# The value at the centre as a column of the slopes' products, two groups' sums taken from PSUM products, and later loads of output weights and queries

## The chip, the cores and the metric

The kernel runs on one core of one Trainium2 chip. The metric is the time of the slowest core on the device, in microseconds (us); here there is only one core. A program has five engines that are used: TensorE (PE, matrix products into PSUM), VectorE (DVE), ScalarE (ACT), GpSimd (POOL) and SyncE (SP, which here only starts transfers). Each engine takes its instructions in the order in which the program holds them, so one that waits holds up all behind it on that engine. Times are those of one profiled execution, unless "runs" are named.

## The reference

The keys and values are one array: `kv` is averaged over 4x4 places (768 keys of 128 channels for each of 4 batches) and multiplied by `w_sr`. Attention runs over 12288 queries a batch, and a feed-forward network follows:

```python
kv_flat = kv_pool.reshape(B, -1, C) @ w_sr          # k = v = kv_flat
s = scale * (q @ k.transpose(0, 2, 1))
a = softmax(s)                                      # over 768 keys
x = a @ v                                           # 49152 tokens x 128
h = x @ w_in                                        # 2048 wide
out = (h - tanh(h)) @ w_out
```

## The kernel before

The outputs of the attention lie close to the mean of the values, so the kernel expands about it. For each batch it pools the keys, takes their mean (the centre, `cen`), and expands `h - tanh(h)` about the centre's `h`: a constant `G0` (128 numbers), a linear part `A` (128x128, "slopes"; kept as an upper and a lower half, `Ah`), and a cubic part of 16 tiles (`Wr` from the output weights, `winr` from the input weights). These come from `about_centre`, once a batch: `first` multiplies the centre by the input weights, a chain of small instructions on a 128x16 tile (`hb`) gives the functions' derivatives, `value` sums G0 (16 products with one column each), `by_first` scales the output weights by the first derivative on POOL (tile `Wg`, four of 128x512), `slopes` multiplies them with the turned input weights `winT` (16 products of 128x128), and `by_third` makes `Wr`.

The tokens go in 96 groups of 512 (24 a batch). For a group, `attention` computes the scores of 768 keys in three parts of 256 (PE into a two-bank tile `big`; ACT takes the exponential, tile `E`; DVE takes off 1 and the score, which leaves a small remainder `r2` in 16 bits). The sum of the three remainders over the keys is needed for the softmax's denominator. It is formed in SBUF by transfers: SP copies the first remainder into `rs` (`copied`), and POOL issues two adding transfers into it (`added`), each waiting for the landing of the one before. Two products with a tile of ones (`shares`) then sum over the keys into a PSUM bank, ACT turns that into the share left (`t`), PE forms the numerator (`straight` and `values`), DVE multiplies (`apart`, tile `df`), and POOL rounds it (`rounded`, tile `dr`). `feed_forward` multiplies `dr` by `winr` (`forth`, eight times two products), ACT squares, DVE cubes (one of eight on ACT and POOL instead), and `back` sums with `Wr`; `result` adds G0.

PSUM is divided into three two-bank tiles `big`, one bank `acc` and one bank `x`. The bank `x` is passed round between the denominator, the numerator and all the small products of `about_centre` and `keys`.

At the start, weights arrive as 64-bit words and are put together on ACT and DVE (`words_of`, eight times 512 KB: four for the input weights `i`, four for the output weights `o`), the first batch's keys arrive in 12 loads of 512 KB (`keys`, pooled by DVE, every third by POOL), and queries in loads of 256 KB. All these are issued by SP. Later batches' keys are gathered by adding transfers during earlier groups.

The order on each engine is not that of the code: every step is entered by `plan.op` with a step number, an engine, an estimated duration, and what it reads and writes, and `Plan.run` builds the order from these. Marks such as `first.{g}` are tiles without memory: they order steps in the plan and put no wait of their own into the program.

Of the kernel before, what the change touches and what calls it, by code (L numbers as in the profile page):

```python
# [21 lines left out]
P = 128  # L22
# [134 lines left out]
def attention_then_ffn(ctx: ExitStack, tc: tile.TileContext, q, kv_by_key, kv_by_place, w_sr, w_in,  # L157
# [18 lines left out]

    BUFS = {"kc": 2, "kvp": 1, "kTr": 2, "vvr": 2, "Mn": 1, "Mh": 2, "A": 2, "Ah": 2, "Wg": 3, "Wr": 2,
            "winr": 2, "q": 4, "qr": 5, "ql": 2, "E": 2, "r2": 7, "rs": 3, "t": 2, "dl": 1, "df": 1, "dr": 2, "u": 3, "r": 4,
            "rp": 2, "v": 2, "z": 1, "o": 2, "row": 2, "col": 2, "G0": 2, "hb": 2, "W2": 1,
# [53 lines left out]
    def words_of(step, load_step, n, kind):  # L233
# [56 lines left out]
        plan.op(load_step, "SP", 0.5, load_words, (), (words,), late=2.0, dma=1.27)  # L290
# [8 lines left out]
    def weights(step, load_step, out_step, load_out):  # L299
# [3 lines left out]
        for n in range(NW):  # L303
            words_of(out_step + n / 8, load_out + n / 8, n, "o")
# [46 lines left out]
    def keys(b, s0):  # L351
# [17 lines left out]
        for j in range(0 if b else NK):  # L369
# [9 lines left out]
            if j % 3 == 2:  # L379
                for k, w in enumerate((8, 4, 2, 1)):  # L380
                    def fold(key=key, w=w, at=at):
                        x = plan[key]
                        to = plan[kvp][:, at].unsqueeze(2) if w == 1 else x[:, :, 0:w]
                        PL.tensor_tensor(out=to, in0=x[:, :, 0:w], in1=x[:, :, w : 2 * w], op=ALU.add)

                    plan.op(s + k / 8, "POOL", 0.2 + KB * w * 0.0021, fold, (key,),
                            ((kvp, j),) if w == 1 else (key,))
            else:
                def pool(key=key, at=at):
                    V.tensor_reduce(out=plan[kvp][:, at], in_=plan[key], op=ALU.add, axis=AX.X)  # L390

                plan.op(s, "DVE", 1.2, pool, (key,), ((kvp, j),))
# [107 lines left out]
    def about_centre(b, s0):  # L500

        cen, hb, G0, Am, Wr, winr = (f"{x}.{b}" for x in ("cen", "hb", "G0", "A", "Wr", "winr"))
        ph, pg, pa = (f"{x}.{b}" for x in ("ph", "pg", "pa"))
# [5 lines left out]
        sb(G0, "G0", [P, 1])  # L509
# [4 lines left out]
        FS, CS, AS, APART, SA, VA, TA, WI, WS = EARLY if b < 2 else LATER  # L514
# [4 lines left out]
        value_at = [known + VA + AS * n if b else n / 2 + VL for n in range(4)]  # L519
        third_at = [known + TA + AS * (n + 0.5) if b else n / 2 - THIRD for n in range(4)]  # L520
        for n in range(4):
            if b or n == 0:
                bank(f"{ph}.{n}", "x" if b else "acc", first_at[n])
            if b:
                bank(f"{pg}.{n}", "x", value_at[n])
                bank(f"{pa}.{n}", "x", slopes_at[n] + APART)
        if not b:
            bank(f"{pa}.0", "acc", slopes_at[0])
            bank(f"{pg}.0", "acc", value_at[0])
# [69 lines left out]
        def sum_value(n):  # L599
            if n:  # L600
                V.tensor_tensor(out=plan[G0], in0=plan[f"{pg}.{n}"][:, 0:1], in1=plan[G0], op=ALU.add)
            else:
                V.tensor_scalar(out=plan[G0], in0=plan[f"{pg}.{n}"][:, 0:1], scalar1=1.0,
                                scalar2=None, op0=ALU.mult)

# [20 lines left out]
        for n in range(4):  # L626
            plan.op(value_at[n], "PE", 0.9, partial(value, n), (gg, ("wout32", n)),
                    (f"{pg}.{n if b else 0}",), late=0.2)
            if b:
                plan.op(value_at[n], "DVE", 0.15, partial(sum_value, n), (f"{pg}.{n}",), (G0,))  # L630
        if not b:
            plan.op(value_at[3], "DVE", 0.15, partial(sum_value, 0), (f"{pg}.0",), (G0,))
# [28 lines left out]
        else:  # L661
            for j in range(2):
                pw = f"pw.{b}.{j}"
                big(pw, winr_at + j / 2)
                for k in range(2):
                    dg = f"dg.{b}.{j}.{k}"
                    sb(dg, "Wg", [P, FW, C], step=winr_at + j / 2 + k / 4)
                    fs = slice((2 * j + k) * FW, (2 * j + k + 1) * FW)

                    def diagonal(j=j, dg=dg, fs=fs):  # L670
                        by = x(8)[:, fs].unsqueeze(2).to_broadcast([P, FW, P])
                        of = ident.unsqueeze(1).to_broadcast([P, FW, P])
                        (PL if j else V).tensor_tensor(out=plan[dg], in0=of, in1=by, op=ALU.mult)

                    def scaled(j=j, k=k, dg=dg, pw=pw):
                        for n in range(FW):
                            f = (2 * j + k) * FW + n
                            at = (k * FW + n) * P
                            PE.matmul(out=plan[pw][:, at : at + P], lhsT=winT[:, f], rhs=plan[dg][:, n],
# [10 lines left out]
        for n in range(NW):  # L690
            wg = f"wg.{b}.{n}"
            fs = slice(n * FW, (n + 1) * FW)
            sb(wg, "Wg", [P, FW, C], step=slopes_at[n])

            def by_first(n=n, wg=wg, fs=fs):
                by = x(4)[:, fs].unsqueeze(2).to_broadcast([P, FW, C])
                PL.tensor_tensor(out=plan[wg], in0=wout32[:, fs], in1=by, op=ALU.mult)

            def slopes(n=n, wg=wg):
                for k in range(FW):  # L700
                    PE.matmul(out=plan[f"{pa}.{n if b else 0}"][:, 0:P], lhsT=winT[:, n * FW + k],
# [3 lines left out]
            def sum_slopes(n=n):  # L705
                of = plan[f"{pa}.{n}"][:, 0:P]
                if n:
                    V.tensor_tensor(out=plan[Am], in0=of, in1=plan[Am], op=ALU.add)
                else:
                    A.copy(out=plan[Am], in_=of)  # L710
# [5 lines left out]
            plan.op(slopes_at[n], "POOL", 1.1, by_first, (gg, ("wout32", n)), (wg,), late=MORE if b else 0.0)  # L716
            joined = slopes_at[n] + (APART if b else SD)
            plan.op(joined, "PE", 0.95, slopes, (wg, "winT"), (f"{pa}.{n if b else 0}",), late=0.2)
            if b and n:
                plan.op(joined, "DVE", 0.29, sum_slopes, (f"{pa}.{n}",), (Am,), late=0.1)  # L720
            elif b or n == 3:
                plan.op(joined, "ACT", 0.3, partial(sum_slopes, 0), (f"{pa}.0",), (Am,), late=0.1)
# [11 lines left out]
        plan.op(joined, "ACT", 0.3, upper_slopes, (Am,), (Ah,), late=0.1)  # L734
# [14 lines left out]
    def attention(g, s0):  # L749
# [21 lines left out]
        behind = (f"first.{g - ago}",) if g >= ago + 3 else ()  # L771
# [25 lines left out]
        sb(rs, "rs", [P, WIDE], F16, step=s0 + AT["copied"])  # L797
# [45 lines left out]
        plan.op(s0 + AT["copied"], "SP", 0.5, copied, (r2s[0],), (rs,), late=2.0, dma=0.6)  # L843
        plan.tile(f"first.{g}", f"first.{g}", 1, lambda: None)
        for k in range(1, AN):
            to = (rs, f"first.{g}") if k == 1 else (rs,)
            plan.op(s0 + AT["added"][k - 1], "POOL", 0.87, partial(added, k), (r2s[k],), to,
                    late=2.4, dma=0.6, lane=True)
        plan.op(s0 + AT["shares"], "PE", 0.455, shares, ("ident", rs), (den,), late=0.196, lane=True)
# [17 lines left out]
    EARLY = (4, 1.6, 7, 3, 5, 4, 9, 18, 8)  # L867
    LATER = (8, 8, 9, 7, 16, 8, 32, 28, 8)
# [3 lines left out]
    def feed_forward(g, s0):  # L872
        b = g // NG
        Ah, Wr, G0, winr, dl, dr = (f"{x}.{k}" for x, k in (
            ("Ah", b), ("Wr", b), ("G0", b), ("winr", b), ("dl", g), ("dr", g)))
# [66 lines left out]
        def result():  # L942
            A.activation(out=plan[o], in_=plan[acc], func=AF.Identity, bias=plan[G0])  # L943
# [4 lines left out]
        plan.op(s0 + AT["result"], "ACT", 0.565, result, (acc, G0), (o,), late=0.16, lane=True)  # L948
# [202 lines left out]
    weights(-LEAD - 50, -LEAD - 60, -17.7, -LEAD - 46)  # L1151
# [4 lines left out]
    VL = -10  # L1156
# [74 lines left out]
```

## Time and profile before

| | us |
|---|---|
| runs, median of 3 | 1346.77 (1346.31 to 1349.07) |
| the profiled execution, its own time | 1346.26 |
| its span in the profile | 1344.5 |
| results of groups 2 to 11, apart | 12.57 each |
| first score product of group 0 begins | 51.19 |
| first `forth` product of group 0 begins | 78.03 |

The span begins with the first instruction and ends with the last; 1.76 us of the execution's own time lie around it. Line numbers are those of the kernel before. A row of the timeline gives the start, the stretch in us, the engine, the line, the operation, what it writes and reads, and how many; in brackets is the idle time of the engine before it and what ended that. Matmul records come two to a product where both sides are f32, one otherwise. The clock column PEclk gives TensorE's granted clock as a share of 2.4 GHz (0.50 is 1.2 GHz).

### The profile page before, as it was taken

Reading aid. Unit: us, or ns where it says so; the run is one execution under the profiler, and the core shown is the slowest. Engines: PE = TensorE matmul, PEld = TensorE weight load, DVE = VectorE, ACT = ScalarE, POOL = GpSimd, SP = SyncE. Lnnn points to the kernel's source line nnn. Section 1 sums busy time; section 2 is a strip of 40 time slices with the busy share of each in tenths; the row PEclk is TensorE's granted clock in tenths of the full one; section 3 lists DMA queues with packets and bytes.
Section 4 is the critical chain, followed back from the end, with each engine's and each line's share of the span. In section 5 each row is a group of like instructions: output and inputs, shape, how many; then the busy total and the mean of one; then the engine's idle time right before and its main releaser. Section 6 shows DMA issues by size and latency. Waiting matters only on the chain.

```text
span 1344.5 us, 17619 instructions
## 1 busy us (share of the span) xinstructions
PE 1279.7 (95%) x5632; PEld 899.7 (67%) x5632; DVE 1221.3 (91%) x1214; ACT 1195.9 (89%) x1403; POOL 1147.4 (85%) x973
## 2 busy tenths in 40 slices
PE   2889999899999999999999999999999999999997
PEld 2657666577666667776666666777676667666664
DVE  6578999888899999998999999899999999899996
ACT  5378999888899999898999999889899999899995
POOL 2568999779999998799999998889998888798896
PEclk7989999999999999999999999999999999999999
DMA  8165666435566664444566664344444444444431
GB/s 345 46 122 119 139 140 132 104 98 135 125 130 138 141 131 109 99 118 107 128 139 132 138 141 114 95 105 109 110 101 104 117 104 102 101 102 106 114 85 35
DMA packets 83574, 160.07 MB, mean 119 GB/s; under 512 B 10032, under 2 KB 12208, under 8 KB 83472
## 3 DMA queue, kind: packets, MB, share of 16 engines
q0 software_dynamic: 34128, 68.04, 31.0%
q1 hardware_dynamic: 49344, 90.81, 19.3%
q8 instruction: 46, 0.75, 0.2%
q14 instruction: 56, 0.46, 0.1%
HBM read 57.93 MB, written 25.39 MB: 62 GB/s over the span
## 4 chain that ended last, share of the span: by engine, by line
PE 45%; POOL 39%; ACT 5%; issue 5%; DMA 3%; DVE 2%; SPq 0%; POOLq 0%; ACTq 0%; DVEq 0%
PE acc L932 13%; PE big L894 12%; POOL rp L912 9%; POOL z L912 9%; PE big L783 6%; POOL rs L805 5%; PE x L825 5%; POOL z L908 4%; POOL ql L819 3%; POOL dr L839 3%; ACT E L787 3%; PE x L815 2%; PE acc L883 2%; POOL dl L863 2%; DMA rs<-r 1%
## 5 line engine op out<-in xcount | busy, mean ns | idle before, releaser
L901 DVE SCALAR_TENSOR_TENSOR r<-big,u 128x1024 fp32r<-128x1024 f32 x672 | 780.6, 1218 | 33.6 <-ACT u L898 32.0
L898 ACT ACTIVATE u<-big 128x1024 f32<-128x1024 f32 x672 | 661.9, 1034 | 45.1 <-PE big L894 34.6
L894 PE MATMUL big<-dr,winr 128*128 128x512 f32 x1536 | 509.6, 413 | 2.5 <-DVE r L790 1.6
L932 PE MATMUL acc<-r,Wr 128*128 128x512 f32 x1344 | 424.7, 408 | 0.7 <-DVE r L901 0.7
L790 DVE SCALAR_TENSOR_TENSOR r<-E,big 128x1024 f16<-128x1024 f32 x288 | 350.3, 1218 | 47.9 <-ACT E L787 44.5
L894 PEld LDWEIGHTS big<-dr,winr 128*128 128x128 f32 x1536 | 275.3, 189 | 97.6 <-DVE r L790 23.1
L787 ACT ACTIVATE E<-big 128x1024 f32<-128x1024 f32 x288 | 295.8, 1029 | 18.7 <-PE big L783 11.4
L932 PEld LDWEIGHTS acc<-r,Wr 128*128 128x128 f32 x1344 | 251.6, 188 | 64.1 <-DVE r L901 1.6
L912 POOL TENSOR_TENSOR rp<-z,v 128x1024 fp32r<-128x1024 f32 x96 | 273.1, 2845 | 0.2
L912 POOL TENSOR_TENSOR z<-z,v 128x1024 f32<-128x1024 f32 x96 | 247.6, 2579 | 4.3
L805 POOL DMA_DIRECT2D rs<-r x192 | 226.4, 1179 | 11.6 <-DMA rs<-r 9.6
L783 PE MATMUL big<-qr,kTr 128*128 128x512 f32 x576 | 196.5, 424 | 1.6 <-ACT v L905 1.6
L839 POOL TENSOR_SCALAR dr<-df 128x512 fp32r<-128x512 f32 x96 | 68.7, 715 | 128.7 <-DVE df L836 92.6
L825 PE MATMUL x<-r,vvr 128*128 128x512 f16 x576 | 176.3, 389 | 0.0
L819 POOL TENSOR_TENSOR ql<-q,qr 128x512 fp32r<-128x512 f32 x96 | 165.0, 1719 | 0.0
L863 POOL TENSOR_TENSOR dl<-df,dr 128x512 fp32r<-128x512 f32 x96 | 164.2, 1711 | 0.0
L783 PEld LDWEIGHTS big<-qr,kTr 128*128 128x128 f32 x576 | 105.5, 190 | 42.9 <-DVE r L790 15.4
L908 POOL TENSOR_SCALAR z<-v 128x1024 f32<-128x1024 f32 x96 | 109.7, 1143 | 0.0
L905 ACT COPY v<-big 128x1024 f32<-128x1024 f32 x96 | 97.6, 1017 | 1.1 <-PE big L894 1.0
L943 ACT ACTIVATE o<-acc,G 128x512 f32<-128x512 f32 x96 | 65.7, 684 | 25.4 <-PE acc L932 24.3
L932 PE MATMUL acc<-rp,Wr 128*128 128x512 f32 x192 | 74.6, 469 | 13.9 <-POOL rp L912 10.1
L825 PEld LDWEIGHTS <-vvr 128*128 128x128 f16 x576 | 33.9, 99 | 79.5 <-issue 79.5
(183 smaller groups left out, 1023.4 us busy)
## 6 DMA issues: line engine op xcount, KB each, us to landing
rs<-r POOLq DMA_DIRECT2D x192, 256.0 KB, 3.9
q<-in_q_dram SPq DMA_DIRECT2D x96, 256.0 KB
rs<-r SPq DMA_DIRECT2D x96, 256.0 KB
out_dram<-o SPq DMA_DIRECT2D x96, 256.0 KB
kvp<-in_kv_by_place_dram POOLq DMA_DIRECT2D x45, 384.0 KB, 4.9
r<-in_kv_by_key_dram SPq DMA_DIRECT2D x6, 512.0 KB
kc<-inverse SPq DMA_DIRECT2D x12, 256.0 KB
u<-in_moe_w_in_dram SPq DMA_DIRECT2D x3, 512.0 KB
```

Source lines behind the costliest of these rows:

```text
L783: PE.matmul(out=half(plan[s], h), lhsT=plan[kTr][:, n * P : (n + 1) * P], rhs=plan[qr], start=True, stop=True)
L787: A.activation(out=plan[e], in_=plan[s], func=AF.Exp)
L790: V.scalar_tensor_tensor(out=plan[r], in0=plan[e], scalar=-1.0, in1=plan[s], op0=ALU.add, op1=ALU.subtract)
L805: PL.dma_start(out=plan[rs], in_=plan[r2s[k]], accum_op=ALU.add)
L819: PL.tensor_tensor(out=plan[ql], in0=plan[qs], in1=plan[qr].bitcast(F32), op=ALU.subtract)
L825: PE.matmul(out=plan[num], lhsT=plan[vvr][:, n], rhs=half(plan[f"r2.{g}.{k}"], h), start=(start and h == 0), stop=(stop and h == 1))
L863: PL.tensor_tensor(out=plan[dl], in0=plan[df], in1=plan[dr].bitcast(F32), op=ALU.subtract)
L894: PE.matmul(out=half(plan[hp], h), lhsT=plan[winr][:, f * P : (f + 1) * P], rhs=plan[dr], start=True, stop=True)
L898: A.activation(out=plan[u], in_=plan[hp], func=AF.Square)
L901: V.scalar_tensor_tensor(out=plan[r], in0=plan[hp], scalar=1.0, in1=plan[u], op0=ALU.add, op1=ALU.mult)
L912: PL.tensor_tensor(out=plan[to], in0=plan[x], in1=plan[y], op=ALU.mult)
L932: PE.matmul(out=plan[acc], lhsT=plan[Wr][:, 2 * n + h], rhs=half(plan[r], h), start=(start and h == 0), stop=(stop and h == 1))
```

## The change

Three edits, all in how the work is cut and ordered.

1. `value` and `sum_value` are gone. `by_first` now scales `winT` instead of the output weights, into tiles `Wg` with rows of 129; the 129th column holds the value function (`beside`, a copy of 128x4 on ACT). `slopes` multiplies with the output weights on the stationary side, so that its products of 128x129 hold the turned slopes and G0 in one tile `At`; a product with the identity (`turn_slopes`) turns the slopes back.
2. Groups 0 and 1 (`DIRECT = 2`) have no `rs`: `shares` runs over the three remainders themselves, six products instead of two.
3. The loads of the output weights and of the first queries stand behind the mark `held`, which the pooling of key load 6 writes; `out_weights` is entered after the keys of batch 0.

```diff
+    DIRECT, HELD = 2, 6
...
-        plan.op(load_step, "SP", 0.5, load_words, (), (words,), late=2.0, dma=1.27)
+        plan.op(load_step, "SP", 0.5, load_words, () if kind == "i" else ("held",), (words,), late=2.0,
+                dma=1.27)
...
-                plan.op(s, "DVE", 1.2, pool, (key,), ((kvp, j),))
+                plan.op(s, "DVE", 1.2, pool, (key,), ((kvp, j), "held") if j == HELD else ((kvp, j),))
...
-        def value(n):
-            for f in range(4 * n, 4 * n + 4):
-                PE.matmul(out=plan[f"{pg}.{n if b else 0}"][:, 0:1], lhsT=wout32[:, f],
-                          rhs=x(3)[:, f : f + 1], start=(f % (4 if b else FT) == 0),
-                          stop=(f % 4 == 3 and (b > 0 or n == 3)))
...
-            sb(wg, "Wg", [P, FW, C], step=slopes_at[n])
+            sb(wg, "Wg", [P, FW, C + 1], step=slopes_at[n])
...
-                PL.tensor_tensor(out=plan[wg], in0=wout32[:, fs], in1=by, op=ALU.mult)
+                PL.tensor_tensor(out=plan[wg][:, :, 0:C], in0=winT[:, fs], in1=by, op=ALU.mult)
+
+            def beside(wg=wg, fs=fs):
+                A.copy(out=plan[wg][:, :, C], in_=x(3)[:, fs])
...
-                    PE.matmul(out=plan[f"{pa}.{n if b else 0}"][:, 0:P], lhsT=winT[:, n * FW + k],
+                    PE.matmul(out=plan[f"{pa}.{n if b else 0}"][:, 0 : C + 1], lhsT=wout32[:, n * FW + k],
...
+        def turn_slopes():
+            PE.matmul(out=plan[pt][:, 0:P], lhsT=plan[At][:, 0:C], rhs=ident, start=True, stop=True)
+
         def upper_slopes():
+            A.copy(out=plan[Am], in_=plan[pt][:, 0:P])
             A.copy(out=plan[Ah][:, 0], in_=plan[Am])
...
-        behind = (f"first.{g - ago}",) if g >= ago + 3 else ()
+        behind = ("held",) if g < ago + 3 else (f"first.{g - ago}",)
...
         def shares():
-            for h in range(2):
-                PE.matmul(out=plan[den], lhsT=share, rhs=half(plan[rs], h), start=(h == 0),
-                          stop=(h == 1))
+            of = [rs] if g >= DIRECT else r2s
+            for n in range(2 * len(of)):
+                PE.matmul(out=plan[den], lhsT=share, rhs=half(plan[of[n // 2]], n % 2),
+                          start=(n == 0), stop=(n == 2 * len(of) - 1))
...
+        if g >= DIRECT:
+            plan.op(s0 + AT["copied"], "SP", 0.5, copied, (r2s[0],), (rs,), late=2.0, dma=0.6)
...
-            A.activation(out=plan[o], in_=plan[acc], func=AF.Identity, bias=plan[G0])
+            A.activation(out=plan[o], in_=plan[acc], func=AF.Identity, bias=plan[At][:, C : C + 1])
...
-    weights(-LEAD - 50, -LEAD - 60, -17.7, -LEAD - 46)
+    weights(-LEAD - 50, -LEAD - 60)
+    plan.tile("held", "held", 1, lambda: None)
...
+        if b == 0:
+            out_weights(-17.7, -LEAD - 46)
```

The order moves in two places. On SP, at the start, this stood before (`in_moe_w_out` are the output weights, `in_q` the queries, `in_kv_by_key` the keys of batch 0, `in_kv_by_place` the first gather of batch 1's keys):

```order
L376 DMA kc<-in_kv_by_key_dram 128x1024
L249 DMA u<-in_moe_w_out_dram 128x4x256
L249 DMA z<-in_moe_w_out_dram 128x4x256
L765 DMA q<-in_q_dram 128x512 x3
L249 DMA u<-in_moe_w_out_dram 128x4x256
L765 DMA q<-in_q_dram 128x512
L249 DMA u<-in_moe_w_out_dram 128x4x256
L376 DMA E<-in_kv_by_key_dram 128x1024
L376 DMA r<-in_kv_by_key_dram 128x1024 x2
L364 DMA kvp<-in_kv_by_place_dram 128x768
```

and this stands there now:

```order
L380 DMA kc<-in_kv_by_key_dram 128x1024
L380 DMA E<-in_kv_by_key_dram 128x1024
L380 DMA r<-in_kv_by_key_dram 128x1024 x2
L250 DMA u<-in_moe_w_out_dram 128x4x256 x3
L250 DMA z<-in_moe_w_out_dram 128x4x256
L756 DMA q<-in_q_dram 128x512 x5
L368 DMA kvp<-in_kv_by_place_dram 128x768
```

The last three key loads have moved ahead of four loads of output weights and four of queries. On PE, from the slopes of batch 0 to the first `values` product of group 0 (`x` is the bank for the denominator, then for the numerator), this stood before:

```order
L783 MATMUL big<-qr,kTr 128x512 x6
L701 MATMUL acc<-Wg,winT 128x128 x16
L809 LDWEIGHTS share
L809 MATMUL x<-rs,share 128x512
L809 LDWEIGHTS share
L809 MATMUL x<-rs,share 128x512
L815 MATMUL x<-qr,Mh 128x512 x2
```

and this stands there now:

```order
L685 MATMUL acc<-Wg,wout_69 128x129 x4
L774 MATMUL big<-qr,kTr 128x512 x2
L802 LDWEIGHTS share
L802 MATMUL x<-r_392,share 128x512
L802 LDWEIGHTS share
L802 MATMUL x<-r_392,share 128x512
...
L802 LDWEIGHTS share
L802 MATMUL x<-r_398,share 128x512
L685 MATMUL acc<-Wg,wout_69 128x129 x8
L808 MATMUL x<-qr,Mh 128x512 x2
```

The shares read the remainders (`r_392`, `r_380`, `r_398`) and no transfer's tile, and twelve of the sixteen slope products now stand behind the score products of group 1 or behind the shares.

## Rows read from the trace of the kernel before

**Rows 1.** SP's timeline at the start (start, stretch, engine, line, operation)
```profile
22.06 0.33 SPq L376 DMA_DIRECT2D E<-in_kv_by_key_dram  x1
```
**Rows 2.** Timeline of DVE and POOL: the last key loads as they land
```profile
20.67 1.22 DVE L390 TENSOR_REDUCE kvp<-kc 128x64 f32<-128x1024 f32 x1 [0.46 <-DMA kc<-in_kv_by_key_dram]
...
29.93 1.22 DVE L390 TENSOR_REDUCE kvp<-E 128x64 f32<-128x1024 f32 x1
...
32.56 2.52 POOL L384 TENSOR_TENSOR r<-r 128x512 f32<-128x512 f32 x3 [9.96 <-DVE kvp L390]
...
36.23 0.15 DVE L429 TENSOR_SCALAR row<-row 128x1 f32<-128x1 f32 x1
```
**Rows 3.** PE's timeline from the keys to the centre's products
```profile
31.30 6.45 PE L410 MATMUL big<-kvp,ident 128*128 128x512 f32 x10 [13.27 <-DVE kvp L390]
...
38.11 3.73 PE L535 MATMUL acc<-col,win 128*128 128x1 f32 x32 [0.25 <-DVE col L439]
```
**Rows 4.** Timeline of all engines: group 0's scores, remainders, and their sum by transfers
```profile
51.19 0.72 PE L783 MATMUL big<-qr,kTr 128*128 128x512 f32 x2
...
54.83 2.35 DVE L790 SCALAR_TENSOR_TENSOR r<-E,big 128x1024 f16<-128x1024 f32 x2 [0.60 <-ACT E L787]
...
57.81 3.73 PE L701 MATMUL acc<-Wg,winT 128*128 128x128 f32 x32
...
59.99 1.02 POOL L805 DMA_DIRECT2D rs<-r  x1
...
65.36 0.88 POOL L805 DMA_DIRECT2D rs<-r  x1 [2.63 <-DMA rs<-r]
...
68.78 1.01 PE L809 MATMUL x<-rs,share 128*128 128x512 f16 x2 [7.25 <-DMA rs<-r]
```
**Rows 5.** The same timeline, on to group 0's first `forth` product
```profile
71.94 2.78 PE L825 MATMUL x<-r,vvr 128*128 128x512 f16 x6
...
74.83 0.69 DVE L836 TENSOR_TENSOR df<-x,t 128x512 f32<-128x512 f32 x1 [13.12 <-PE x L825]
...
75.61 0.62 POOL L839 TENSOR_SCALAR dr<-df 128x512 fp32r<-128x512 f32 x1 [6.30 <-DVE df L836]
...
78.03 0.70 PE L894 MATMUL big<-dr,winr 128*128 128x512 f32 x2 [1.22 <-DVE r L790]
```
**Rows 6.** Stretches: length, busy of PE, PEld, DVE, ACT, POOL, then clock, transfers
```profile
45.50:65.80 20.30, 15.93 (x127) 14.99 (x126) 9.69 (x15) 10.91 (x15) 13.70 (x15) 1.00 0.25 72
...
65.90:76.10 10.20, 6.63 (x15) 3.35 (x15) 0.69 (x1) 1.60 (x3) 3.90 (x5) 0.50 0.64 117
```
**Rows 7.** Chain of waits: start, length, engine, what; two products at full clock
```profile
84.18 0.45 PE x L825 x2
```
**Rows 8.** Groups by line: putting weights together on DVE (busy, mean ns)
```profile
L275 DVE SCALAR_TENSOR_TENSOR wout<-u,v 128x512 int32<-128x512 int32 x3 | 2.1, 691 | 0.1
...
L268 DVE TENSOR_SCALAR v<-v 128x512 f32<-128x512 f32 x8 | 3.4, 421 | 7.4 <-ACT v L265 7.4
```
**Rows 9.** Forms of lines L673, L697, L655: count, then ns min/median/max
```profile
L673 DVE TENSOR_TENSOR Wg<-ident,hb x2: 693/1112/1530, 45.0 to 45.6; 128x512 f32<-128x512 f32 x2
...
L697 POOL TENSOR_TENSOR Wg<-wout,hb x16: 1037/1418/1839, 54.1 to 945.6; 128x512 f32<-128x512 f32 x16
...
L655 POOL TENSOR_TENSOR winr<-win,kc x12: 1856/2168/2623, 331.3 to 959.8; 128x512 fp32r<-128x512 f32 x12
```
**Rows 10.** Groups by line, batches 1 to 3: `value`'s products, a small copy
```profile
L595 PE MATMUL x<-hb,wout 128*128 128x1 f32 x96 | 11.9, 245 | 0.6 <-DVE df L836 0.4
...
L710 ACT COPY A<-x 128x128 f32<-128x128 f32 x3 | 0.8, 267 | 1.1 <-PE x L701 1.1
```
**Rows 11.** Stretches, as in rows 6: one group of batch 1's preparation
```profile
346.80:362.20 15.40, 14.08 (x69) 10.31 (x68) 13.17 (x14) 12.46 (x15) 15.40 (x15) 1.00 0.59 128
```
**Rows 12.** DVE's timeline: the longest row of cubes between two other instructions
```profile
1037.38 8.06 DVE L901 SCALAR_TENSOR_TENSOR r<-big,u 128x1024 fp32r<-128x1024 f32 x7
```

More of the change, by code (lines that the diff above doesn't have):

```diff
@@ L297, in words_of, with out_weights, weights @@
         plan.op(step, "DVE", 0.66, add, (part, rs), (part,), port=True)
-    def weights(step, load_step, out_step, load_out):
+    def out_weights(step, load_step):
+        for n in range(F // WN):
+            words_of(step + n / 8, load_step + n / 8, n, "o")
+    def weights(step, load_step):
         NW = F // WN
@@ L625, in about_centre @@
             plan.op(s0 - 5, on, 1.1, third_order, (hb,), (hb, a3s))
[L626 to L632, printed above, removed]
         NW, FW = 4, FT // 4
@@ L678, in scaled @@
                             at = (k * FW + n) * P
-                            PE.matmul(out=plan[pw][:, at : at + P], lhsT=winT[:, f], rhs=plan[dg][:, n],
+                            PE.matmul(out=plan[pw][:, at : at + P], lhsT=winT[:, f], rhs=plan[dg][:, n, 0:C],
                                       start=True, stop=True)
@@ L705, in sum_slopes @@
             def sum_slopes(n=n):
-                of = plan[f"{pa}.{n}"][:, 0:P]
+                of = plan[f"{pa}.{n}"][:, 0 : C + 1]
                 if n:
-                    V.tensor_tensor(out=plan[Am], in0=of, in1=plan[Am], op=ALU.add)
+                    V.tensor_tensor(out=plan[At], in0=of, in1=plan[At], op=ALU.add)
                 else:
-                    A.copy(out=plan[Am], in_=of)
+                    A.copy(out=plan[At], in_=of)
             def by_third(n=n, fs=fs):
@@ L714, in by_third @@
                 PL.tensor_tensor(out=plan[Wr][:, fs], in0=wout32[:, fs], in1=by, op=ALU.mult)
-            plan.op(slopes_at[n], "POOL", 1.1, by_first, (gg, ("wout32", n)), (wg,), late=MORE if b else 0.0)
+            plan.op(slopes_at[n], "POOL", 1.1, by_first, (gg, "winT"), ((wg, 0),), late=MORE if b else 0.0)
+            plan.op(slopes_at[n], "ACT", 0.2, beside, (gg,), ((wg, 1),), late=0.1)
             joined = slopes_at[n] + (APART if b else SD)
-            plan.op(joined, "PE", 0.95, slopes, (wg, "winT"), (f"{pa}.{n if b else 0}",), late=0.2)
+            plan.op(joined, "PE", 1.0, slopes, (wg, ("wout32", n)), (f"{pa}.{n if b else 0}",), late=0.2)
             if b and n:
-                plan.op(joined, "DVE", 0.29, sum_slopes, (f"{pa}.{n}",), (Am,), late=0.1)
+                plan.op(joined, "DVE", 0.29, sum_slopes, (f"{pa}.{n}",), (At,), late=0.1)
             elif b or n == 3:
-                plan.op(joined, "ACT", 0.3, partial(sum_slopes, 0), (f"{pa}.0",), (Am,), late=0.1)
+                plan.op(joined, "ACT", 0.3, partial(sum_slopes, 0), (f"{pa}.0",), (At,), late=0.1)
             plan.op(third_at[n], "POOL", 1.25, by_third,
                     (a3s, ("wout32", n)), ((Wr, n),), port=True)
+        def turn_slopes():
+            PE.matmul(out=plan[pt][:, 0:P], lhsT=plan[At][:, 0:C], rhs=ident, start=True, stop=True)
         def upper_slopes():
+            A.copy(out=plan[Am], in_=plan[pt][:, 0:P])
             A.copy(out=plan[Ah][:, 0], in_=plan[Am])
@@ L733, in about_centre @@
         joined = slopes_at[3] + (APART if b else 1) + 0.1
-        plan.op(joined, "ACT", 0.3, upper_slopes, (Am,), (Ah,), late=0.1)
+        bank(pt, "x" if b else "acc", joined)
+        plan.op(joined, "PE", 0.25, turn_slopes, (At, "ident"), (pt,), late=0.2)
+        plan.op(joined, "ACT", 0.65, upper_slopes, (pt,), (Am, Ah), late=0.1)
         plan.op(joined, "POOL", 0.35, lower_slopes, (Am, Ah), (Ah,))
@@ L796, in attention @@
         rs = f"rs.{g}"
[L797 removed]
+        if g >= DIRECT:
+            sb(rs, "rs", [P, WIDE], F16, step=s0 + AT["copied"])
         bank(den, "x", s0 + AT["shares"])
@@ L842, in attention @@
         r2s = [f"r2.{g}.{k}" for k in range(AN)]
-        plan.op(s0 + AT["copied"], "SP", 0.5, copied, (r2s[0],), (rs,), late=2.0, dma=0.6)
         plan.tile(f"first.{g}", f"first.{g}", 1, lambda: None)
[L845 to L849, printed above, removed]
+        if g >= DIRECT:
+            plan.op(s0 + AT["copied"], "SP", 0.5, copied, (r2s[0],), (rs,), late=2.0, dma=0.6)
+            for k in range(1, AN):
+                to = (rs, f"first.{g}") if k == 1 else (rs,)
+                plan.op(s0 + AT["added"][k - 1], "POOL", 0.87, partial(added, k), (r2s[k],), to,
+                        late=2.4, dma=0.6, lane=True)
+        plan.op(s0 + AT["shares"], "PE", 0.455 if g >= DIRECT else 1.36, shares,
+                ["ident"] + ([rs] if g >= DIRECT else r2s), (den,), late=0.196, lane=True)
         plan.op(s0 + AT["left"], "ACT", 0.49, share_left, (den,), (t,), late=0.14, lane=True)
```

36 lines of the change are left out of this document (12 added, 24 removed).

## The prediction

> **What bounds the kernel now.** I read the page first: PE is busy for 95% of the span, DVE 91%, ACT 89%, POOL 85%. With groups 12.57 us apart there is no engine to relieve cheaply in the steady part, so I went to the two kinds of place where an engine waits: the first 80 us and the preparation of batches 1 to 3.
>
> At the start the chain of waits runs through transfers twice. First the keys. Key load 9 is pooled at 20.67, but the next one pooled, load 6, starts at 29.93, and the last one on POOL at 32.56 [rows 2], since SP issued the first of those three only at 22.06 [rows 1], behind output weights and queries. The keys' mean is there at 36.38 (36.23 + 0.15), PE has run ten warming products from 31.30 to 37.75, and the centre goes through the input weights at 38.11 [rows 2, 3]. Second the sum of group 0's remainders. These are done at 57.18 [rows 4]; PE takes its next product for group 0 at 68.78, after 7.25 us of waiting for the adding transfers, issued at 59.99 and 65.36. From there a short chain leads to the first `forth` product at 78.03 [rows 5], and PE did that work at a granted clock of 0.50, where it had 1.00 before it fell idle [rows 6].
>
> In the preparation of the later batches POOL is what is full: in one such group it is busy for all of 15.40 us, PE for 14.08 [rows 11].
>
> **Part 1: keys before output weights and queries.** Between loads 9 and 6 lie four loads of output weights (512 KB each) and four of queries (256 KB each). They took the time from 20.67 to 29.93 less the one load that follows: loads 6, 10 and 11 land 1.30 and 1.33 apart (29.93; 31.23, when DVE is ready for the second; 32.56), so 9.26 - 1.3 = 8.0 us [rows 2]. All are issued by SP, and they land in the order of issue, so the three key loads land 8.0 earlier: 21.9, 23.2, 24.5. DVE reaches them in time (it ends load 9 at 21.89) [rows 2]. POOL's last fold, mean, warming products and centre then shift as one; the warming products need load 6, so they shift too. I take nothing for the clock there, but PE stands idle 13.27 us before them now [rows 3] and some 5 then; the step from 0.50 to 1.00 could fall up to 1.3 us later against them (three products at 0.43 more).
>
> What is late next: putting the output weights together. On DVE it was done in gaps before the mean; now two instructions of 0.42 and one of 0.69 [rows 8] stand before the centre's copy: the mean's end at 28.4, these, and the copy make 30.2, where the products by the input weights would start at 38.11 - 8.0 = 30.1, so 0.1 is lost; the rest fills DVE's waits for PE. So group 0's scores begin at 51.19 - 7.9 = 43.3. Between its remainders stand two more of 0.42 each, of which ACT's pace (0.60 of waiting before the second remainder [rows 4]) hides all but 0.2. Remainders done: 57.18 - 8.0 + 0.2 = 49.4, or **7.8 earlier**.
>
> **Part 2: groups 0 and 1 without the transfers' sum.** From 57.18 to 78.03 are 20.85 us now. In the new order, from 49.4, PE takes in turn: four slope products at 0.93 (16 took 3.73) [rows 4], two score products 0.46, six share products at 0.227 (two take 0.45 at full clock) [rows 7] = 1.36, and eight slope products 1.86. For the last four of these POOL must have scaled the third tile: it first waits for the third part of the output weights, which DVE ends at 49.4 + 0.69 + 0.42 + 0.69 = 51.2 (the adding instruction taken like the 0.69 of rows 8), then makes `Wr` and `Wg` at 1.04 each [rows 9]: 53.3. So slopes end at 54.2; three `straight` 0.7 and six `values` 1.36 make 56.25; DVE's `df` 0.69 and POOL's `dr` 0.62 [rows 5] make 57.6. PE meanwhile takes four score products, four slopes and two scores (0.92 + 0.93 + 0.46 = 58.6), waits for ACT's copy of `At` (0.27 [rows 10]), and turns it: about 59.3. That is the first `forth` product: 9.9 us instead of 20.85, **10.95 earlier**. On POOL `dr` stands behind the last `Wg`, a `ql` and the last `Wr`, which end about 57.0, so it does not wait.
>
> This goes by full clock, as in the stretch 45.50 to 65.80, where PE was busy 15.93 of 20.30 us [rows 6]. At 0.50 the streamed products in it (scores 4 x 0.46, shares and values 1.36 each, `straight` 0.7: 5.2 us) would take 5.2 more: the lower bound of this part is 5.7 earlier.
>
> **Part 3: what comes back.** Group 1's shares are four products more: +0.9. The copies of `At` and `A` (0.27 each) stand on ACT in the way of the first squares: +0.5. DVE and POOL hold each other up where both take two inputs from SBUF: the same DVE product took 0.69 alone and 1.53 beside POOL [rows 9]. Two conversions now fall among POOL's products: between 0 and 2 x 0.84 on each, and I take +0.7. By the Trainium skill (SBUF — State Buffer, section "SBUF: two separate sides") the two share a pair of ports that one instruction holds to its end while the other blocks fully. The trace agrees (0.69 and 1.53); by that rule every meeting costs a whole instruction, and the four late conversions of 0.69 would hold POOL up by 2.8, which makes the sum below -15.3. From the other side, the clock: after 78.03 PE had more time at 0.50 that should now be at 1.00; I take 0.75 back, out of 0 to 1.5.
>
> **Part 4: batches 1 to 3.** Taken away: 96 matmul records at 245 ns over three batches, 4.0 us a batch on PE [rows 10], four small DVE sums, and four passages through the bank `x`. Added: a product to turn (two records, 0.5 at most), a passage through `x`, ACT copies. On PE that is some 3.6 a batch, but the chain there runs through POOL, whose work is the same in number. So 0; the bounds are -3.6 x 3 = -11 (PE the bound throughout) and POOL's price for rows of 129: twelve products at 1418 ns in the median, and the nearest kind with strides, L655, takes 2168 [rows 9], so up to +0.75 x 12 = +9. I stay with 1418, since L655 strides over single elements and here only whole rows of 128 lie apart. Some POOL products of batches 2 and 3 come a group later in the new order, which shifts POOL's work and not its sum.
>
> **Sum.** -7.8 - 10.95 + 0.9 + 0.5 + 0.7 - 0.75 = -17.4. The profiled execution took 1346.26, which gives 1328.9; it lies 0.5 below the median of the runs (1346.77), so I predict 1329.
>
> **Rivals.**
> (a) *The second stall only shrinks.* PE's clock falls in its short waits between scores (it waits for ACT's rounding of group 1's queries) and part 2 gives 5.7, or POOL is late with `dr` by its two longer products. For it: 0.50 in the stretch from 65.90 on [rows 6]. Against: that came after 7 us of idling, the new waits are under 2. Time: 1328.9 + 5.2 + 1 = 1335; range 1333 to 1340.
> (b) *The loads don't move.* `held` puts no wait into the program, only the order of SP's queue; if the loads shared the bandwidth, the keys would land as before, and only parts 2 and 3 remain: 1328.9 + 7.8 = 1337. Against: the landings above follow the order of issue one by one.
> (c) *PE is the bound in the later batches after all.* Then part 4 gives half to all of its 11: 1318 to 1323. For it: PE is busy 14.08 of 15.40 there; against: POOL is busy 15.40 of 15.40 [rows 11].
> (d) *Slower: the turning product waits on DVE.* In batches 1 to 3 `turn_slopes` stands on PE a few products behind the last slopes and needs DVE's sum into `At`; DVE can have seven cubes ahead of it, 8.06 us [rows 12], with all of PE's queue and the bank `x` behind. Three times 8 is 24: 1328.9 + 24 = 1353. It decides the sign above 5.8 us a batch. Against: in the new order one remainder and one cube stand between DVE's `df` and that sum, not seven cubes: some 2.4 us, beside which PE has three pairs of products to do.
>
> **How the numbers follow.** Forecast 0.60, with its own range 1324 to 1333; (a) 0.17; (b) 0.05; (c) 0.15; (d) 0.03. Between 1319 and 1338 lie the forecast, (b), two thirds of (c) and half of (a) at least: above 0.8. A difference of 0.2% (2.7 us) is about what a measurement here can tell. All cases but (d) and a sum of the worst of (a) and the strided price are faster by more: 0.95; within 0.2%: 0.02; slower: 0.03.
>
> **What would show it.** Right: the last key fold on POOL starts near 24.5, the warming products near 23.3; group 0's shares start within 2 us of its last remainder; the first `forth` product is near 60, at a granted clock of 1.00 from about 40 on; the time between results in steady groups stays 12.57 and the preparation groups keep their sum within 2 us a batch. Wrong: a wait before `dr` on POOL, a clock of 0.50 between 48 and 60, or PE waiting for DVE before the turning product.

## The result: 1328.1 us, predicted 1329

| | before | changed |
|---|---|---|
| runs, median | 1346.54 (1345.14 to 1349.07, 4 runs) | 1328.13 (1326.40 to 1328.89, 4 runs) |
| ratio | | 0.9861, 95% interval 0.9845 to 0.9877 |
| again, beside other kernels | 1347.20 (11 runs) | 1327.18 (5 runs), 0.985, 0.9837 to 0.9864 |
| span of the profiled execution | 1344.5 | 1326.8 |

The time lies 0.9 below the forecast, but that is luck in part: two errors of 4.4 and 4.7 us that cancel are in it. Read from the results of single groups (the ACT instruction that adds G0), the changed kernel is ahead by this much:

| result of group | 0 | 11 | 24 | 43 | 67 | 95 | end of span |
|---|---|---|---|---|---|---|---|
| before | 97.3 | 239.6 | 427.1 | 681.3 | 996.1 | 1336.9 | 1344.5 |
| changed | 84.3 | 226.4 | 413.8 | 666.4 | 979.5 | 1320.3 | 1326.8 |
| ahead by | 13.0 | 13.2 | 13.3 | 14.9 | 16.6 | 16.6 | 17.7 |

The prediction has 17.4 at group 0 and nothing behind it. It was 13.0 there (4.4 short); 1.6 and 1.7 came in the preparation of batches 2 and 3, and 1.1 between the last result and the end (with what the rounding leaves, 4.7 not foreseen).

These are the rows of the changed kernel that answer to [rows 2, 3]: timeline of DVE, POOL and PE around the last keys.

```profile
22.07 1.22 DVE L394 TENSOR_REDUCE kvp<-E 128x64 f32<-128x1024 f32 x1
...
23.44 7.51 PE L414 MATMUL big<-kvp,ident 128*128 128x512 f32 x10 [5.22 <-DVE kvp L394]
...
24.69 2.54 POOL L388 TENSOR_TENSOR r<-r 128x512 f32<-128x512 f32 x3 [1.92 <-DVE kvp L394]
...
28.17 0.15 DVE L433 TENSOR_SCALAR row<-row 128x1 f32<-128x1 f32 x1
...
31.31 3.73 PE L536 MATMUL acc<-col,win 128*128 128x1 f32 x32 [0.25 <-DVE col L443]
```

The keys landed where they were forecast (22.07 for 21.9, 24.69 for 24.5), and the mean was there at 28.32 (28.4). Only the centre's products are 1.1 late: the ten warming products took 7.51 instead of 6.45, at the low clock (first row of the stretches below).

The next rows answer to [rows 4, 5]: the same timeline from group 0's scores to its first `forth` product.

```profile
43.99 0.71 PE L774 MATMUL big<-qr,kTr 128*128 128x512 f32 x2
...
46.75 2.27 POOL L678 TENSOR_TENSOR Wg<-winT,hb 128x512 f32<-128x512 f32 x2
46.94 2.37 DVE L272 TENSOR_SCALAR v<-v 128x512 int32<-128x512 int32 x1
...
49.56 2.34 DVE L781 SCALAR_TENSOR_TENSOR r<-E,big 128x1024 f16<-128x1024 f32 x2
...
54.42 2.62 PE L802 MATMUL x<-r,share 128*128 128x512 f16 x6
...
59.37 1.47 PE L818 MATMUL x<-r,vvr 128*128 128x512 f16 x6
...
60.94 0.69 DVE L829 TENSOR_TENSOR df<-x,t 128x512 f32<-128x512 f32 x1 [2.10 <-PE x L818]
...
61.73 0.62 POOL L832 TENSOR_SCALAR dr<-df 128x512 fp32r<-128x512 f32 x1 [1.77 <-DVE df L829]
...
63.49 0.49 PE L712 MATMUL acc<-ident,At 128*128 128x128 f32 x2 [0.36 <-ACT At L694]
...
63.76 0.70 PE L889 MATMUL big<-dr,winr 128*128 128x512 f32 x2
```

The second row from the top and the one under it are the point. A conversion of output weights (L272) that takes 0.42 or 0.43 alone began on DVE 0.19 behind the first of two POOL products and ended 0.29 behind the second: 2.37. Two remainders of group 0 stood behind it on DVE, so they ended at 51.90, not 49.4. Then six share products took 2.62 instead of 1.36. The stretches (columns as in [rows 6]) say why:

```profile
18.00:29.50 11.50, 6.28 (x10) 2.55 (x10) 8.73 (x17) 3.42 (x5) 7.21 (x13) 0.55 1.06 403
...
40.00:49.80 9.80, 7.52 (x52) 6.13 (x52) 5.67 (x12) 7.73 (x13) 6.48 (x7) 1.00 0.38 77
50.00:56.70 6.70, 5.87 (x18) 3.79 (x19) 6.70 (x8) 3.16 (x4) 3.18 (x4) 0.50 0.01 3
57.00:64.00 7.00, 6.64 (x43) 5.09 (x42) 4.14 (x6) 3.60 (x7) 3.76 (x4) 1.00 0.15 40
```

PE had waits of 0.66, 1.62 and 1.03 among its scores, and from 50.0 to 56.7 its granted clock was 0.50 (1.2 GHz).

### The profile page after: what moved, and what is told of

The parts are those of the page before. It is cut to its first block, busy times and chain, and to the rows that moved or that the text cites. A ratio compares the mean times of both kernels' runs of the same rounds, so it can differ in the third digit from the quotient of the medians.

```text
span 1326.8 us, 17379 instructions
## 1 busy us (share of the span) xinstructions
PE 1271.4 (96%) x5520; PEld 889.0 (67%) x5520; DVE 1220.6 (92%) x1201; ACT 1197.4 (90%) x1423; POOL 1143.5 (86%) x969
## 4 chain that ended last, share of the span: by engine, by line
POOL 44%; PE 38%; ACT 6%; issue 6%; DMA 2%; DVE 2%; SPq 0%; POOLq 0%; ACTq 0%; DVEq 0%
PE acc L927 11%; POOL rp L907 11%; PE big L889 10%; POOL z L907 10%; POOL rs L797 6%; PE big L774 5%; POOL z L903 4%; PE x L818 4%; POOL ql L812 3%; POOL dr L832 3%; ACT E L778 3%; PE x L808 2%; PE acc L878 2%; ACT v L900 2%; POOL kvp L366 1%
## 5 line engine op out<-in xcount | busy, mean ns | idle before, releaser
L797 POOL DMA_DIRECT2D rs<-r x188 | 223.7, 1190 | 6.9 <-DVE r L896 4.7
L774 PEld LDWEIGHTS big<-qr,kTr 128*128 128x128 f32 x576 | 105.9, 191 | 44.7 <-DVE r L781 13.3
L938 ACT ACTIVATE o<-acc,At 128x512 f32<-128x512 f32 x96 | 65.7, 684 | 30.4 <-PE acc L927 29.7
```

What stands on the lines that cost most here:

```text
L774: PE.matmul(out=half(plan[s], h), lhsT=plan[kTr][:, n * P : (n + 1) * P], rhs=plan[qr], start=True, stop=True)
L797: PL.dma_start(out=plan[rs], in_=plan[r2s[k]], accum_op=ALU.add)
```

## The experiments

They were run in three sets, each beside the kernel before on one chip, and on another chip each time: the four kernels of the first paragraph, the four of the second, and the last four. The kernel before took 1347.54, 1347.20 and 1346.96 there; across sets the ratios to it compare best. Medians are of 4 to 6 runs each. "Ahead" and "g0" (the result of group 0) are read from one profile of each kernel; two profiles of the changed kernel differ by 1.6 us at g0 (84.3 and 82.7).

**Each edit alone, and all without edit 1.** The diffs are the three parts of the change as shown; without edit 1, `value` and the old `slopes` stay.

> Edit 3 alone in the kernel before (the loads of output weights and first queries behind key load 6; group sums by transfers and the value's own products stay). Theory: the three keys land 8 us earlier and the scores of group 0 begin near 44 (they began at 51.19, and at 43.99 with all three edits), and everything behind them shifts by as much, since the adding transfers of groups 0 and 1 stay: 1339 to 1340. Rival (the edits need each other): POOL's scaling of the output weights needs the late weights here, so it pushes POOL's adding transfers back and less than 4 us come through: 1342.5 or more.

1340.17 (ratio 0.9944, 0.993 to 0.9959), 7.4 below the kernel before: the theory in time. The scores of group 0 begin at 45.5 and not near 44, the first `forth` product at 71.1 (78.03).

> Edit 2 alone in the kernel before (groups 0 and 1 take six share products from the three remainders, no transfers). Theory of the prediction: the wait of 7.25 us and what leads to it go, first forth product 8 to 11 us earlier than 78.03, less 0.9 given back: 1336.5 to 1339. Rival from the trace of the changed kernel (its part behind the scores became only 7 us shorter, with a granted clock below 1.00 in it): 1340 to 1341.

1336.89 (0.9933, 0.9917 to 0.9949): the theory. From the last remainder to the first `forth` product it takes 12.2 instead of 20.85.

> Edit 1 alone in the kernel before (the value at the centre as a 129th column, turned slopes). Theory from the trace of the changed kernel: batch 1 is unchanged, batches 2 and 3 give 1.6 us each, and the start stays within 1 us: 1342.5 to 1344. Rival, the prediction's own term of nothing for batches 1 to 3 (the 3.3 us seen there came from the other edits by way of the order): 1346 to 1347.

1340.84 (0.9947, 0.9932 to 0.9961): more than either said. In its trace it is 1.9 ahead at group 0, loses 0.6 in batch 1, gains 1.3 in batch 2 and 1.7 in batch 3, and ends 1.1 sooner behind the last result.

> Edits 2 and 3 without edit 1. Theory that the three edits add up: the changed kernel less what edit 1 gives alone, so 3.3 us above it, 1331 to 1332. Rival: without edit 1 POOL must scale the output weights themselves, which now come last, so the slopes of batch 0 and with them the first result come later still: 1333.5 or more, with PE waiting for Wg on POOL between 55 and 65.

1326.35 (0.9851, 0.9834 to 0.9869): both were wrong. The three edits alone give 7.4, 10.7 and 6.7, together 24.7; all three give 18 to 20, and two of them 21. In this kernel the same conversion stands ahead of the remainders, they end at 49.4, and group 0's result is at 81.9.

**The changed kernel again, and three that undo a part of it.** `hybrid` takes edit 1 back for batch 0 only:

```
-                PL.tensor_tensor(out=plan[wg][:, :, 0:C], in0=winT[:, fs], in1=by, op=ALU.mult)
+                PL.tensor_tensor(out=plan[wg][:, :, 0:C], in0=(winT if b else wout32)[:, fs], in1=by, op=ALU.mult)
...
+            for n in range(4):
+                plan.op(n / 2 + VL, "PE", 0.9, partial(value, n), (gg, ("wout32", n)), (pg,), late=0.2)
```

> The changed kernel once more, as the measure for the other three of this set. Theory that edit 1 costs about 2.4 us in batch 0 beside edits 2 and 3 (first result at 84.3 with it, at 81.9 without it): 1327.5 to 1329. Rival that its distance to the kernel without edit 1 (1326.35) was chance: 1326 to 1327.

1327.18: between the two; the runs overlap those without edit 1 (1325.34 to 1328.59).

> All three edits, but batch 0 sums its value and slopes in the old way; batches 1 to 3 use the 129th column. On every engine the first 130 instructions stand as in the kernel without edit 1. Theory (edit 1 costs 2.4 us in batch 0 and gives 1.6 in batch 3): 1324 to 1325.5, at least 2 below the changed kernel, first result near 82. Rival (edit 1 does nothing measurable anywhere): within 1 us of the changed kernel.

1327.33 (0.9853, 0.9839 to 0.9867): in time the rival. The trace shows both of the theory's parts, g0 at 80.8 (82.7 in the changed kernel of this set) and batch 3's gain, and a loss between groups 67 and 95 that no edit touches (below).

`no_sum` sets `DIRECT = 0`; `no_loads` takes the mark `held` and the late `out_weights` out.

> Edits 1 and 3, with the transfers' sum kept for groups 0 and 1. Theory (the second stall comes back in full behind earlier keys): the shares of group 0 start 11 us or more behind its last remainder, and the time is 8 to 10.6 us above the changed kernel, 1336 to 1338.5. Rival (edit 1 covers part of the stall, since slopes no longer wait): 1333 to 1335.

1337.62 (0.9925, 0.9911 to 0.9938), 10.4 above: the theory. Remainders end at 49.6, the first share product begins at 61.73, behind the transfer (timeline):

```profile
59.43 1.54 POOL L797 DMA_DIRECT2D rs<-r  x1
...
61.73 1.01 PE L802 MATMUL x<-rs,share 128*128 128x512 f16 x2 [2.36 <-DMA rs<-r]
```

> Edits 1 and 2, with the loads as before. Theory (the keys land 8 us later again): 7 to 8 us above the changed kernel, 1335 to 1336.5, scores of group 0 at 51 to 52. Rival (earlier keys were partly given back by the conversions of output weights that now fall among group 0's remainders): only 3 to 5 us above it, 1331 to 1333.

1338.58 (0.9933, 0.992 to 0.9946), 11.4 above: more than the theory, and the rival is out. Most of the excess lies ahead of the scores. They begin at 53.1, 9.5 behind the 43.6 of the changed kernel in this set; from there to the first `forth` product (72.65) it takes 19.5 us against 19.2. POOL scales all four pieces of `Wr` in a row here ahead of three of `Wg`, but PE does not wait for that; its one long wait in this stretch is for ACT's rounding of the queries (timeline). Why the scores come later than the 51 to 52 expected was not told apart.

```profile
52.16 4.04 POOL L697 TENSOR_TENSOR Wr<-wout,hb 128x512 fp32r<-128x512 f32 x4
...
58.26 2.93 PE L773 MATMUL big<-qr,kTr 128*128 128x512 f32 x6 [3.08 <-ACT qr L758]
```

**Lock or clock.** The order was written out and single instructions moved in it, everything else staying in its place:

```
+        for name, ahead_of in self.moves:
+            at = order.pop(next(k for k, (_, i) in enumerate(order) if i == self.names[name]))
+            order.insert(next(k for k, (_, i) in enumerate(order) if i == self.names[ahead_of]), at)
...
+    plan.moves += [("shift.o.2", "beyond.0.1"), ("within.o.3", "beyond.0.1")]     (moved, both)
...
+        PE.matmul(out=plan["fill"], lhsT=ident, rhs=winT[:, 0:4].rearrange("p t c -> p (t c)"),
+                  start=True, stop=True)                                          (filled, both: six times)
```

> The changed kernel with two DVE conversions of output weights (0.43 us each alone) taken from between group 0's remainders to ahead of the first of them; every other instruction on every engine stays in its place. Theory (what the prediction missed at the remainders is that one of them waits for POOL's two scalings, 2.37 us beside them): last remainder of group 0 at 49.5 instead of 51.5 to 51.9, first forth product 1 to 2 us earlier, 1325.5 to 1326.5. Rival (PE waits there for POOL's third scaling, which hangs on the output weights): the remainders come earlier, the first forth product does not, 1327 to 1328.

1324.76 (0.9829, 0.9816 to 0.9843; 1322.76 to 1325.47): the theory, and better than it. All five runs lie below the five of the changed kernel in the set above (1325.84 to 1328.34, ratio 0.985), though on another chip. The first `forth` product is 4.0 earlier than there, where 1 to 2 were expected; 0.6 of that stood at the first score already. Its timeline:

```profile
40.39 0.42 DVE L275 TENSOR_SCALAR v<-v 128x512 int32<-128x512 int32 x1
...
45.74 2.26 POOL L681 TENSOR_TENSOR Wg<-winT,hb 128x512 f32<-128x512 f32 x2
46.62 2.35 DVE L784 SCALAR_TENSOR_TENSOR r<-E,big 128x1024 f16<-128x1024 f32 x2 [0.61 <-ACT E L781]
...
50.44 1.47 PE L806 MATMUL x<-r,share 128*128 128x512 f16 x6
...
55.95 0.69 DVE L833 TENSOR_TENSOR df<-x,t 128x512 f32<-128x512 f32 x1
...
56.99 0.62 POOL L836 TENSOR_SCALAR dr<-df 128x512 fp32r<-128x512 f32 x1
...
58.77 0.70 PE L893 MATMUL big<-dr,winr 128*128 128x512 f32 x2
```

The conversion takes 0.42 now. Beside the same pair of POOL products stand two remainders, and these are not held up (2.35 for two): of their two inputs one lies in PSUM. From there on the prediction's schedule holds to within half a microsecond: remainders 48.97 (49.4), shares 50.44 (50.8), `df` 55.95, `dr` 56.99 (57), first `forth` 58.77 (59.3). And in this trace the clock stayed up, with nothing done for it (stretches):

```profile
37.00:49.00 12.00, 8.82 (x64) 7.56 (x63) 7.61 (x15) 9.15 (x16) 7.79 (x8) 1.00 0.30 64
49.00:59.00 10.00, 9.64 (x60) 7.09 (x59) 9.20 (x11) 6.33 (x11) 7.20 (x7) 1.00 0.12 29
```

> The changed kernel with six products more on PE (128x512, f32, into the bank x, used by nothing) in its three waits between the scores of groups 0 and 1; all else in its place. Theory (rival a of the prediction was half true: PE's waits there let the clock fall to 0.50 in 48 to 57, and PE ends that stretch): the clock stays at 1.00 from 40 to 60, six share products take 1.5 instead of 2.62, first forth product 1.5 to 3 us earlier, 1324.5 to 1326. Rival (the stretch hangs on DVE and POOL, so the clock is of no account): clock up, first forth product within 0.7 us, 1327 to 1328.

1326.42 (0.9844, 0.983 to 0.9858), between theory and rival and within the noise of the changed kernel. The clock did stay at 1.00 (row of its stretches, then two of its timeline), and six shares take 1.47, but the conversion is still held and the first `forth` product is at 62.14, 0.65 before that of the changed kernel in the set above. Counted from the first score it is 18.1 us, against 19.2 there and 19.8 in the profile under the result, so 1.1 to 1.7 less:

```profile
49.00:62.00 13.00, 12.64 (x67) 8.50 (x66) 11.84 (x15) 6.55 (x12) 7.34 (x8) 1.00 0.17 39
```

```profile
47.02 2.37 DVE L275 TENSOR_SCALAR v<-v 128x512 int32<-128x512 int32 x1
...
53.96 1.47 PE L806 MATMUL x<-r,share 128*128 128x512 f16 x6
...
62.14 0.69 PE L893 MATMUL big<-dr,winr 128*128 128x512 f32 x2
```

> Both of these edits together: the two conversions ahead of the remainders, and six filling products. Theory (lock and clock are the two causes of the start's missing 3 to 4 us, and add up): last remainder at 49.5, clock at 1.00, first forth product at 60 or before, 1323 to 1325. Rival (one hides the other): no better than the better of the two.

1326.00 (0.9841, 0.9828 to 0.9855): the rival, and worse than `moved` alone in the trace. With the wait gone the filling products are in the way: the shares begin 2.35 later than in `moved` (timeline).

```profile
52.79 1.47 PE L807 MATMUL x<-r,share 128*128 128x512 f16 x6
...
60.98 0.69 PE L894 MATMUL big<-dr,winr 128*128 128x512 f32 x2
```

So the held conversion is what made the remainders late. With it moved, and the one behind it, they take 5.99 again instead of 7.9, and the first `forth` product comes 15.8 us behind the first score instead of 19.2. The 1.9 at the remainders are shown by that. The other 1.5, behind them, go with the clock, and what kept it up is not shown. In the three traces with the conversion held and nothing filled in (the changed kernel twice, and `value_kept` below) it fell for as long as in the stretch 50.00 to 56.70 above. But `no_sum` has no conversion held there, remainders that end in time, the same waits of PE (0.66 and 1.62, as in `moved`) and the same busy time of PE in the 6.0 us before, and its clock fell all the same, for half as long. These are PE's row behind the second wait and two stretches of `no_sum`, then the same of `moved`:

```profile
48.65 1.64 PE L774 MATMUL big<-qr,kTr 128*128 128x512 f32 x4 [1.62 <-ACT qr L759]
```

```profile
43.00:49.00 6.00, 3.72 (x24) 2.73 (x23) 3.01 (x3) 5.54 (x9) 6.00 (x8) 1.00 0.00 0
49.20:52.60 3.40, 3.40 (x13) 3.06 (x12) 2.77 (x4) 2.14 (x3) 0.78 (x2) 0.50 0.20 77
```

```profile
48.05 1.19 PE L777 MATMUL big<-qr,kTr 128*128 128x512 f32 x4 [1.62 <-ACT qr L762]
```

```profile
42.40:48.40 6.00, 3.72 (x24) 2.73 (x23) 3.01 (x3) 5.45 (x8) 5.60 (x7) 1.00 0.29 44
48.40:51.80 3.40, 3.40 (x21) 2.38 (x20) 3.40 (x6) 2.09 (x4) 1.21 (x2) 1.00 0.21 39
```

So a held conversion is not needed for the clock to fall here, and one trace of `moved` does not show that moving it keeps the clock up. Nor do `filled` and `both` price the clock by itself, since the filling products stand in PE's way.

**Where batches 2 and 3 gained.**

```
+        for n in range(4 if b else 0):
+            value_at = known + (4 if b < 2 else 8) + AS * n
+            bank(f"pg.{b}.{n}", "x", value_at)
+            plan.op(value_at, "PE", 0.0, partial(value, n), (gg, ("wout32", n)), (f"pg.{b}.{n}",))
```

> The changed kernel with the value's 16 products put back on PE for batches 1 to 3 (their result is used by nothing); DVE, ACT, POOL and SP are untouched. Theory (the 1.7 us that batch 3 gave, and about 1 of batch 2, are PE's time, so PE was the bound there): from the result of group 43 to that of 67 it takes 314.6 again instead of 313.1, 2.5 to 4 us more in all, 1329.5 to 1332. Rival (POOL bounds these stretches as the prediction took it, and the gain came from the order of POOL's pieces): 313.1 stays, 1327 to 1328.5.

1328.31 (0.9861, 0.9846 to 0.9876): the rival's number, and yet not its reason. From group 43 to 67 it took 313.64 (before 314.73, changed 313.06): 0.6 of the 1.7 came back. These are the rows for groups 55 to 67 (columns as in [rows 6]), of before, the changed kernel and this one:

```profile
832.00:996.10 164.10, 161.98 (x754) 117.27 (x752) 151.53 (x157) 148.22 (x177) 147.09 (x132) 1.00 0.42 103
```

```profile
817.00:979.50 162.50, 159.81 (x724) 114.38 (x722) 150.57 (x153) 148.81 (x182) 146.91 (x132) 1.00 0.43 104
```

```profile
816.10:979.30 163.20, 162.25 (x756) 117.82 (x754) 151.35 (x153) 148.58 (x182) 147.04 (x132) 1.00 0.42 104
```

PE is busy for 98.7% of this stretch in the kernel before and POOL for 89.6%, so PE is the nearest to a bound here. The nine profiles with edit 1 and without the products give 162.2 to 162.8 for it, the four without edit 1 163.9 to 164.3; so this gain is edit 1's. The products themselves are worth some 0.7 of these 1.6, by one profile that lies 0.3 above the highest of the nine. But PE's work alone does not set the length: with the products kept PE is busy for 162.25, no less than the 161.98 before, and the stretch is still 0.9 shorter. For this 0.9 the four DVE sums and the four passages of the bank `x` remain, which this kernel doesn't put back, and that wasn't told apart. In batch 2 the same stretch (groups 36 to 43) took 94.8 in the changed kernel, 96.4 with the products kept, and between 94.9 and 96.5 in kernels without edit 1, so its 1.6 can't be given to one edit.

## Why the prediction came out right

**Part 1 (7.8 earlier).** Right in mechanism: the landings, the order of SP's queue and the mean are within 0.2 us, and rival (b) is out. The scores came 7.2 earlier, not 7.9, for the clock in the warming products, which the text had priced at up to 1.3; of the rest the next point tells.

**Between the remainders.** This is the step that failed: "Between its remainders stand two more of 0.42 each, of which ACT's pace ... hides all but 0.2". With them it took 7.91 from the first score to the last remainder, against 5.99 before: 1.9 lost, not 0.2. The prediction counted the meetings of DVE and POOL only where DVE takes two inputs from SBUF. The trace has a DVE instruction with one input that waited through two POOL products. The kernel's own plan could have said so: it enters `within` and `shift` with `port=True`, and `Plan.run` lets no such instruction start beside one of POOL's by its estimates; in the trace they met all the same. The Trainium skill (SBUF — State Buffer, section "SBUF: two separate sides") counts a DVE instruction in a two-port mode among those that need the shared pair, as well as one with two SBUF inputs; the 2.37 beside POOL and the 0.42 alone agree with that; that the conversion runs in such a mode is not shown by a run. The prediction quoted this section and used half of its rule.

**Part 2 (10.95 earlier).** Measured 9.0: from the last remainder to the first `forth` product it takes 11.9 instead of 9.9 us, at a granted clock of 0.50 from 50.0 to 56.7. That is the prediction's own sign of being wrong, a clock of 0.50 between 48 and 60; the first `forth` product came at 63.76 and not near 60, and the shares 2.5 behind the last remainder, not within 2. Rival (a) had named the fall of the clock and put it down to PE's waiting for ACT's rounding. That wait of 1.62 is in `moved`, where the clock stays up, and in `no_sum`, where it falls without a held remainder, so this ground of the rival is not ruled out; with the remainders held the low clock lasted longer. `moved` covers the same way at full clock in 9.8, so the terms of this part were right.

**Part 3 (0.9 + 0.5 + 0.7 - 0.75 = 1.35 given back).** Measured 1.2: from the first `forth` product to the result of group 0 it takes 20.5 us against 19.3.

**Part 4 (nothing).** Right for batch 1 (0.1), 1.6 and 1.7 short in batches 2 and 3. The price of 0 was read from one group of batch 1 [rows 11], where POOL is full, and carried to batches whose preparation is spread out further (results there are at most 15.3 apart, in batch 1 up to 18.05); there PE is nearly full, and rival (c) is true in part: 3.3 came of its 11. POOL's product into rows of 129 took 1509 ns in the mean where the product before took 1402 (the longest 2102, above the 1839 of [rows 9]), so the strided price of 750 each did not come. Rival (d) did not show: the turning products of batches 1 to 3 waited 0.7 for DVE in all. Groups by line (busy, mean ns, idle before and its releaser), one of the kernel before and two of the changed one:

```profile
L697 POOL TENSOR_TENSOR Wg<-wout,hb 128x512 f32<-128x512 f32 x16 | 22.4, 1402 | 1.8 <-PE acc L701 1.8
...
L678 POOL TENSOR_TENSOR Wg<-winT,hb 128x512 f32<-128x512 f32 x16 | 23.8, 1509 | 0.0
...
L712 PEld LDWEIGHTS x<-ident,At 128*128 128x128 f32 x6 | 1.0, 188 | 0.8 <-DVE At L692 0.7
```

**The sum.** -5.3 at the last remainder and -9.0 behind it make -14.3 at the first `forth` product; +1.2 to the first result, -3.5 from there to the last (3.3 of it in batches 2 and 3) and -1.1 behind it make the span's -17.7. The forecast of -17.4 was met by luck, because the later batches and the end brought what the start lost. The -1.1 is not explained: from the last result to the end it takes 6.4 to 6.9 in nine of the 14 profiles and 7.4 to 7.6 in five, and no edit parts them: edit 1 alone is among the nine, edit 1 with either of the others among the five.

## What to carry to other kernels

When one engine's instructions are moved among another's, look at what each of them will stand beside, not only at how long it takes alone: two instructions of 0.42 us in the wrong place cost some 2.4 us of the whole, the clock's fall included. Price a stage from its own rows: a bound read in one batch's preparation did not hold for the next one, whose work is spread differently. And when a stall and a low clock are seen together, take each away by itself, and look for the same waits in the other traces before one is called the cause of the other: here one trace kept its clock without the stall, and another lost it.

## What was not expected of the hardware

- A DVE instruction that waits for POOL can wait through two of its instructions: 2.37 us beside two POOL products in a row (2.27 together) for the 0.42 that it takes alone, in all four traces in which it stands there (2.37 three times, 2.38 once).
- At one place of the program the granted clock falls for a short while in some executions and not in others. Some 160 us behind the result of group 67 PE waits 2.8 us for POOL in all 14 traces (the first two rows, PE's timeline of the changed kernel and of the one without edit 1). In ten of them the clock falls about the end of this wait, in four it does not; what decides is not shown. (At the head of batch 1 PE waits some 3.0 us, and there the clock falls in all 14.) From group 67 to 95, where no edit changes anything, it took 339.2 to 339.5 us in the four, 340.7 to 341.0 in seven with a short fall, and 342.0 to 342.2 in three with a longer one. The other rows are stretches, of the kernel without edit 1, the changed one and `hybrid`:

```profile
1141.87 0.98 PE L927 MATMUL acc<-rp,Wr 128*128 128x512 f32 x2 [2.80 <-POOL rp L907]
```

```profile
1140.88 0.73 PE L940 MATMUL acc<-rp,Wr 128*128 128x512 f32 x2 [2.77 <-POOL rp L920]
```

```profile
978.60:1317.80 339.20, 334.81 (x1430) 232.39 (x1428) 327.77 (x301) 321.00 (x373) 294.00 (x237) 1.00 0.40 99
```

```profile
979.50:1320.30 340.80, 336.42 (x1430) 233.85 (x1428) 327.81 (x301) 320.80 (x373) 294.08 (x237) 0.99 0.40 99
```

```profile
977.40:1319.40 342.00, 337.62 (x1430) 235.21 (x1428) 327.79 (x301) 320.77 (x373) 293.94 (x237) 0.99 0.40 98
```

This is as large as the differences between several of the kernels here, so that between `hybrid`, the changed kernel and the one without edit 1 no order is shown.
